# Gate and up products of two token chunks as a 2x2 block product with seven half-depth products in place of eight

## The chip, the cores and the metric

One core of one Trainium2 chip runs the whole program. The metric is device time in microseconds (us): the median of several executions. Beside it stands one profiled execution, whose records every row below comes from. The engines are PE (TensorE matmul; PEld is its weight load), DVE (VectorE), ACT (ScalarE), POOL (GpSimd) and SP (SyncE, which issues the DMAs here). A matmul accumulates into one of eight PSUM banks of 128 x 512 floats.

## The reference

A pre-norm transformer block with 2048 tokens, model width 448, 16 heads of 28, a sliding attention window of 256, and a gated feed-forward of width 1792:

```python
x = A_x                                   # (1, 2048, 448)
h = x + attention(layernorm(x), A_wqkv, A_wo)
n = layernorm(h)
g = n @ B_w_gate                          # 448 -> 1792
u = n @ B_w_up                            # 448 -> 1792
out = h + (gelu_tanh(g) * u) @ B_w_down   # 1792 -> 448
```

## The kernel before, in words

**High and low parts.** Every float32 operand is held as two rounded parts, `hi` and `lo = x - hi` (`to_hi` on ACT, `to_lo` on DVE or POOL), and a product is the sum of hi·hi, lo·hi and hi·lo. The model width 448 is three blocks of 128 rows and one of 64. `xT` holds the normalised tokens with the model width on the partitions: blocks 0 to 2 hi, block 3 with the last 64 rows' hi in one half and their lo in the other, blocks 4 to 6 lo. `TERMS` lists the eleven pairs (weight part, weight block, token block) that make one product of a 128-wide tile of `B_w_gate` or `B_w_up` with a chunk of 512 tokens:

```python
TERMS = [(0, 0, 0), (0, 1, 1), (0, 2, 2), (0, 3, 3), (0, 0, 4), (0, 1, 5), (0, 2, 6),
         (1, 0, 0), (1, 1, 1), (1, 2, 2), (1, 3, 3)]
```

**The attention stage** projects q, k, v, computes scores, takes maxima, exponentials and the weighted sum, and ends with the output projection (`output`). `attend` (L894) runs its matmuls in column tiles of 32 (`tile_position=(0, 32 * j)`), everything else in that stage on the full array.

**The feed-forward stage** (`feed_forward`, `product`) has 56 products: 14 tiles of the feed-forward width times 4 chunks of 512 tokens, in groups of 3, 4, 4 and 3 tiles (`GROUPS`). A product computes gate and up for its tile and chunk (two banks), then gelu (ACT, L1125), the gating product (DVE, L1127), the hi and lo parts of the result (`proj`), and the down product: for each of four blocks of 128 tokens three terms of 448 columns, accumulated over the group in four banks, and at the end of a group added to `hres` (L1158).

- The first four products (`n < PAIRED`) are done "whole": 2 x 11 matmuls over 128 partitions and 512 columns. They are also what fills the end of the attention stage.
- The other 52 are done "paired": each matmul over 128 partitions is cut into two halves of 64 rows with `tile_position` (0, 0) and (64, 0), of which one works for the gate bank and one for the up bank at the same time (`pair`). Phase 0 has ten such pairs and phase 1, with the halves exchanged, eleven, since a term of only 64 rows then takes its place beside another one: 21 pairs in place of 22 whole matmuls. The down products of all 56 but the last are paired too, 12 pairs each, in two phases of six.
- Two halves that work at the same time must write different banks. Where a bank changes from one half to the other, `seen` (L1068, tile `word`) makes ACT read one element of the bank after the last matmul of the first half, and the first matmul of the other half waits for that.
- In the paired stretch the two phases of a gate/up product alternate with the two phases of an earlier down product, so that a phase lies between one `seen` and the matmul that waits for it. `feed_forward` writes this order out by a chain of dependencies.

**Order.** All instructions are recorded first (`Lists.op`, with a cost, a latency and a key), and a planner (`Lists.refine`, a random search with `SEED` and `ROUNDS`, then `Lists.run`) writes out one order for each engine. Its costs know nothing of tile modes. `mul` (L484) issues nearly all matmuls, `to_hi` is L487 and `to_lo` L490, so rows are told apart by tiles and shapes. Weights of a tile arrive by one DMA and are cut in hi and lo into one of seven slots (`RECS`): two in `proj`, one in `rq`, two in `rk`, two in `rec`. So `xT,rk` in a row of the profile is a gate/up product whose weights lie in `rk`, and `rec,proj` a down product with weights in `rec`.

Of the kernel before, what the change touches and what calls it, by code (L numbers as in the profile page):

```python
# [25 lines left out]
GROUPS = [3, 4, 4, 3]  # L26
REC = 2944
NB = NG * CS
# [12 lines left out]
LEAD = 110  # L41
# [3 lines left out]
SWAP = -60  # L45
# [3 lines left out]
AHEAD = 7  # L49
BEHIND = 5  # L50
# [3 lines left out]
PAIRED = 4  # L54
MOVED = 0
SPANS = {"pp", "proj", "raw", "xT", "h", "rqf", "rkf", "vm", "rec0", "rec1", "rec2"}
# [13 lines left out]
ROUNDS = 220  # L70
SEED = 33
# [295 lines left out]
def block_kernel(ctx: ExitStack, tc, x, wqk_in, wv_in, wo_in, ffn_in, out):  # L367
# [16 lines left out]
    xT = pool.tile([128, 7, S], F32R, name="xT")  # L384
    rq_m = pool.tile([128, 4096], F32R, name="rq")
    rk_m = pool.tile([128, 6144], F32R, name="rk")
# [7 lines left out]
    last_hi = pool.tile([128, 128], F32R, name="lasthi")  # L394
# [28 lines left out]
    def open_rec():  # L423
        fst.close()
        p = ctx.enter_context(tc.tile_pool(name="fp", bufs=1))
        rec.extend(p.tile([128, REC], F32R, name=f"rec{i}") for i in range(2))
        rec.append(p.tile([128, S], F32R, name="xh"))


    rq = [rq_m[:, 2048 * u:2048 * u + 2048].rearrange("p (j t) -> p j t", j=4) for u in range(2)]  # L430
# [141 lines left out]
    def turn(t, key):  # L572
        c = slice(t * 128, (t + 1) * 128)
        d = xn_d[t]
        xb, at = (v_m[:, REC:REC + D], span("vm", REC, D)) if t > 7 and t % 2 else (xn[1], ("xn", 1))
        op("dve", 0.56, 0.65, key, lambda: nc.vector.transpose(xb, xn[0]), [("xn", 0)], [at], port=True)
        for a in range(4):
            dst = d.rearrange("(b i) t -> i b t", i=32)[:, :, 32 * a:32 * a + 32]
            src = xb[32 * a:32 * a + 32].rearrange("i (b t) -> i b t", t=32)
            dma(key, 150, lambda dst=dst, src=src: nc.sync.dma_start(dst, src), [at], [("xnd", t, a)])  # L580
        put = [("xnd", t, a) for a in range(4)]
# [13 lines left out]
        op("act", 0.7, 0.82, key + 0.2, hi, [("xt3", t)], [XT(t), "lasthi"])  # L595
        op("dve", 0.75, 0.82, key + 0.2, lo, [XT(t), "lasthi"], [XT(t)], port=True)
# [357 lines left out]
    def flat(m, name, o):  # L954
# [5 lines left out]
    RECS = [(lambda o=o, m=m, name=name: flat(m, name, o), flat(m, name, o)[1], need) for m, name, o, need in (  # L960
        (proj_m, "proj", 0, None), (proj_m, "proj", REC, None), (rq_m, "rqf", 0, "ringfree"),
        (rk_m, "rkf", 0, "ringfree"), (rk_m, "rkf", REC, "ringfree"))] + \
        [(lambda i=i: flat(rec[i], f"rec{i}", 0), flat(rk_m, f"rec{i}", 0)[1], "fp") for i in range(2)]
    GH = [(proj_m, 2 * REC + 1024 * i) for i in range(2)]
    NR = len(RECS)
# [8 lines left out]
    def weight_at(i):  # L974

        q = 0 if i < 3 else i % 3
        raw, at0, name = raw_m[:, 0:1472], 0, "raw"
        if q:
            raw, at0, name = v_m[:, 1472 * (q - 1):1472 * q], 1472 * (q - 1), "vm"
        return raw, at0, name  # L980
# [5 lines left out]
    def weight_splits(i, key, after=()):  # L986
        raw, at0, name = weight_at(i)
        cut = ((0, 512), (512, 512), (1024, D))
        get, rat, opened = RECS[i % NR]
# [16 lines left out]

    def feed_forward():  # L1010
        first = [4 * sum(GROUPS[:gi]) + k for gi, gn in enumerate(GROUPS) for k in range(gn)]
        loaded = split = -1
        n = 0
        for gi, gn in enumerate(GROUPS):
            for c in range(4):
                down = [Bank(("down", i)) for i in range(4)]
                for k in range(gn):
                    i = sum(GROUPS[:gi]) + k
                    while loaded < 2:
                        loaded += 1  # L1020
                        split += 1
                        weights(loaded, 16 * NB + 5 * loaded if loaded < 2 else FFN + 30 * first[loaded] - 20)
                    if n == PAIRED:
                        for cc in (1, 2, 3, 0):
                            cs = slice(512 * cc, 512 * cc + 512)
                            dma(FFN + 30 * PAIRED - 25 + cc, 128, lambda cs=cs: nc.sync.dma_start(
                                f(rec[2][64:128, cs]), f(xT[0:64, 3, cs])), [span("xT", 4 * cc, 4), "fp"], [("xh", cc)])
                    product(n, i, c, k, gn, gi, down)
                    while split < NF - 1 and first[split + 1] <= n + BEHIND:
                        split += 1  # L1030
                        weight_splits(split, FFN + 30 * first[split] - 20, phase[n][0][0:1])
                    while loaded < NF - 1 and first[loaded + 1] <= n + AHEAD:
                        loaded += 1
                        if loaded < 3:
                            split += 1
                            weights(loaded, FFN + 30 * first[loaded] - 20, phase[n][0][0:1])
                        else:
                            weight_load(loaded, FFN + 30 * first[loaded] - 20, phase[n][0][0:1])
                    n += 1

        todo = [h for m in range(n) for h in (down_a[m], down_b[m])]
        order = [todo.pop(0) for _ in range(4)]
        for m in range(PAIRED, n):
            for ph in phase[m]:
                order += [ph, todo.pop(0)]
        order += todo
        order = [o for part in order for o in part]
        for o, last in zip(order, [None] + order):
            for d in [last] if last else whole:
                if d not in o.deps:  # L1050
                    o.deps.add(d)
                    d.users.append(o)

    row = {}
    down_a, down_b, phase, whole = {}, {}, {}, []
    HALF = (slice(0, 64), slice(64, 128))

    def pair(key, n, lat, a, b, r, banks):

        def go():  # L1060
            for x, (bk, w, m, start, stop) in enumerate((a(), b())):
                mul(bank[bk.k][:, 0:n], w, m, start=bool(start), stop=bool(stop),
                                 tile_position=(64 * x, 0), skip_group_check=True)
        return op("pe", mm(n), lat, key, go, r, (), banks)

    def seen(key, b):

        op("act", 0.08, 0.17, key, lambda: nc.scalar.activation(word[0:1, 0:1], bank[b.k][0:1, 0:1], AF.Copy), (),  # L1068
           (), b)

    def product(n, i, c, k, gn, gi, down):
        get, rat, _ = RECS[i % NR]
        key = FFN + 30 * n
        toks = slice(c * 512, (c + 1) * 512)
        early = n < EARLY
        paired = n >= PAIRED
        bs = []
        for q in range(0 if paired else 2):

            turn = 2 * (n - EARLY) + q + (2 if n == 2 else -2)  # L1080
# [4 lines left out]
            for a, (h, wb, xb) in enumerate(TERMS):  # L1085
                whole.append(op("pe", mm(512), 0.403, key + (SWAP if n == 3 else 0) + q * NP + a / NP, lambda a=a, h=h, wb=wb, xb=xb, q=q, b=b: mul(
                    bank[b.k], get()[0][q][h][:, wb, :], xT[:, xb, toks], start=(a == 0), stop=(a == NP - 1)),
                   [span("xT", 4 * c, 4), *rat[q][h]], (), b, tag="early" if early else None))
        if paired:
# [226 lines left out]
```

## Time and profile before

| what | us |
|---|---|
| median of 3 runs (698.36 to 698.57) | 698.57 |
| the profiled execution's own time | 698.08 |
| its span, first to last instruction | 696.4 |
| PE busy | 687.8 (99%) |
| DVE, ACT, POOL busy | 396.9, 362.4, 158.7 |
| granted TensorE clock, mean | 0.999 |

The span is what the rows of the trace divide up; 1.68 us lie around it. A busy share of an engine is an average over stages: POOL, for instance, is idle in nearly all of the feed-forward stage. A matmul's row gives its start and a modelled duration that is longer than the distance to the next start, since matmuls are pipelined; the price of one is therefore read from the distance between the starts of rows. Two halves of a pair start together and are two instructions.

### The profile page before, as it was taken

Reading aid. Unit: us, or ns where it says so; the run is one execution under the profiler, and the core shown is the slowest. Engines: PE = TensorE matmul, PEld = TensorE weight load, DVE = VectorE, ACT = ScalarE, POOL = GpSimd, SP = SyncE. Lnnn points to the kernel's source line nnn. Section 1 sums busy time; section 2 is a strip of 40 time slices with the busy share of each in tenths; the row PEclk is TensorE's granted clock in tenths of the full one; section 3 lists DMA queues with packets and bytes.
Section 4 is the critical chain, followed back from the end, with each engine's and each line's share of the span. In section 5 each row is a group of like instructions: output and inputs, shape, how many; then the busy total and the mean of one; then the engine's idle time right before and its main releaser. Section 6 shows DMA issues by size and latency. Waiting matters only on the chain.

```text
span 696.4 us, 15402 instructions
## 1 busy us (share of the span) xinstructions
PE 687.8 (99%) x5897; PEld 604.7 (87%) x5897; DVE 396.9 (57%) x1057; ACT 362.4 (52%) x930; POOL 158.7 (23%) x253
## 2 busy tenths in 40 slices
PE   8999999999999999999999999999999999999997
PEld 8998888888888887778899999999999999999996
DVE  7987877876687978877764232245232244333224
ACT  7658767776767888896653222234222234222221
POOL 5604434344454653753100000000000000000000
PEclk9999999999999999999999999999999999999999
DMA  8888647475556688524663000012100000001012
GB/s 297 262 282 243 210 150 229 141 213 164 176 168 197 160 247 226 157 55 95 146 188 131 1 2 2 1 44 88 45 1 2 1 1 2 1 1 55 10 45 106
DMA packets 83138, 79.12 MB, mean 114 GB/s; under 512 B 34104, under 2 KB 72952, under 8 KB 83064
## 3 DMA queue, kind: packets, MB, share of 16 engines
q1 hardware_dynamic: 83064, 78.14, 37.4%
q8 instruction: 46, 0.75, 0.4%
q14 instruction: 28, 0.23, 0.1%
HBM read 48.23 MB, written 29.36 MB: 111 GB/s over the span
## 4 chain that ended last, share of the span: by engine, by line
PE 91%; ACT 3%; DVE 3%; issue 1%; POOL 1%; DMA 0%; DVEq 0%; ACTq 0%
PE bank L484 85%; PE bank L894 5%; PE bank L542 1%; ACT pp L864 1%; ACT xn L537 1%; ACT xT L487 1%; DVE bnst L519 1%; ACT rq L487 0%; DVE xT L490 0%; DVE mt L792 0%; DVE hres L941 0%; POOL bnve L511 0%; PE bank L819 0%; DMA hres<-in_x_dram 0%; ACT proj L487 0%
## 5 line engine op out<-in xcount | busy, mean ns | idle before, releaser
L484 PE MATMUL bank<-xT,proj 64*128 64x512 f32 (+1 forms) x907 | 177.1, 381 | 0.0
L792 DVE CUSTOM_DVE_ANT_0 mt<-bank,mt 128x384 bf16<-128x384 f32 (+2 forms) x256 | 129.4, 528 | 34.4 <-PE bank L484 29.4
L864 ACT ACTIVATE pp<-bank 128x384 f32<-128x384 f32 (+2 forms) x352 | 124.1, 390 | 44.8 <-PE bank L484 39.1
L484 PEld LDWEIGHTS bank<-xT,proj 64*128 64x128 f32 (+1 forms) x907 | 118.6, 188 | 11.9 <-issue 0.8
L1127 DVE TENSOR_TENSOR mt<-bank,mt 128x512 f32<-128x512 f32 x54 | 37.2, 688 | 129.3 <-ACT mt L1125 129.3
L875 POOL TENSOR_SCALAR_AFFINE_SELECT pp<-pp 128x512 f32<-128x512 f32 x120 | 75.6, 643 | 114.3 <-ACT pp L864 109.6
L484 PE MATMUL bank<-rq,rk 104*128 104x384 f32 (+2 forms) x352 | 97.3, 297 | 0.8 <-ACT pp L864 0.4
L1125 ACT ACTIVATE mt<-bank 128x512 f32<-128x512 f32 x54 | 32.2, 596 | 108.5 <-PE bank L484 108.5
L484 PE MATMUL bank<-rk,rq 84*128 84x384 f32 (+2 forms) x256 | 81.5, 333 | 0.6 <-DVE proj L490 0.5
L1068 ACT ACTIVATE word<-bank 1x1 f32<-1x1 f32 x162 | 25.4, 157 | 106.7 <-PE bank L484 106.4
L484 PEld LDWEIGHTS bank<-rq,rk 104*128 104x128 f32 x352 | 65.5, 189 | 14.3 <-ACT pp L864 4.0
L484 PE MATMUL bank<-xT,rk 64*128 64x512 f32 x656 | 77.7, 376 | 0.0
L484 PE MATMUL bank<-xT,rec 64*128 64x512 f32 x656 | 77.7, 376 | 0.0
L484 PEld LDWEIGHTS bank<-xT,rec 64*128 64x128 f32 x656 | 63.6, 186 | 7.2
L484 PEld LDWEIGHTS bank<-xT,rk 64*128 64x128 f32 x656 | 63.6, 186 | 7.2
L1158 DVE TENSOR_TENSOR hres<-bank,hres 128x448 f32<-128x448 f32 x64 | 35.5, 617 | 59.5 <-ACT mt L1125 33.8
L484 PE MATMUL bank<-proj,xT 128*128 128x224 f32 x352 | 58.0, 275 | 0.0
L490 DVE TENSOR_TENSOR proj<-mt,proj 128x512 fp32r<-128x512 f32 x54 | 37.3, 692 | 35.7 <-ACT proj L487 30.7
L484 PEld LDWEIGHTS bank<-rk,rq 84*128 84x128 f32 x256 | 48.1, 190 | 8.3 <-issue 2.9
L484 PEld LDWEIGHTS bank<-proj,xT 128*128 128x128 f32 x352 | 51.8, 191 | 0.9
L484 PE MATMUL bank<-wos,ohl 128*128 128x448 f32 x192 | 51.4, 365 | 0.2 <-DVE mx L792 0.2
L487 ACT ACTIVATE proj<-mt 128x512 fp32r<-128x512 f32 x54 | 34.0, 629 | 31.0 <-DVE mt L1127 30.0
(109 smaller groups left out, 967.6 us busy)
## 6 DMA issues: line engine op xcount, KB each, us to landing
rk<-k SPq DMA_DIRECT2D x44, 336.0 KB
rq<-q SPq DMA_DIRECT2D x32, 336.0 KB
q<-proj SPq DMA_DIRECT2D x15, 448.0 KB
raw<-in_ffn_dram SPq DMA_DIRECT2D x7, 736.0 KB
v<-in_ffn_dram SPq DMA_DIRECT2D x7, 736.0 KB
k<-proj SPq DMA_DIRECT2D x11, 448.0 KB
hres<-in_x_dram SPq DMA_DIRECT2D x16, 224.0 KB
out_dram<-hres SPq DMA_DIRECT2D x16, 224.0 KB
```

Source lines behind the costliest of these rows:

```text
L484: nc.tensor.matmul(o.rearrange("p (t h) -> p t h", h=2), w, mixed(m), **how)
L487: nc.scalar.activation(dst, src, AF.Copy)
L490: (eng or nc.vector).tensor_sub(dst, src, f(hi))
L519: op("dve", 0.65, 0.63, key(t), lambda t=t: nc.vector.bn_stats(bnst[t % 2], hres[:, t, :]), [HR(t)], [("bnst", t % 2)])
L792: nc.vector.tensor_tensor_reduce(plain(junk[s % 2][:, o:384]), unmixed(bank[b.k][:, o:384]), plain(mask[:, o:384]), 1.0, -BIG, OP.add, OP. ...
L864: nc.scalar.activation(plain(pp[:, j, o * 128:o * 128 + n]), unmixed(bank[b.k][:, 0:n]), AF.Exp, scale=SCALE)
L875: nc.gpsimd.affine_select(a, a, pattern=[[0, 4], [-cm, 128]], compare_op=op_, fill=0.0, base=0, channel_multiplier=cm)
L894: nc.tensor.matmul(bank[b.k][32 * j:32 * j + DH + 1, lo * 128:(hi + 1) * 128], v[:, 4 * c - 2 + m, g % 2, j, :], pp[:, j, at[m] * 128:(at[ ...
L1068: op("act", 0.08, 0.17, key, lambda: nc.scalar.activation(word[0:1, 0:1], bank[b.k][0:1, 0:1], AF.Copy), (), (), b)
L1125: op("act", 0.485 + table, 0.608 + table, key + NP, lambda: nc.scalar.activation(plain(g2), src(0), AF.Gelu_apprx_tanh), held[0], G2, bs[0 ...
L1127: op("dve", 0.605, 0.702, key + 2 * NP, lambda: nc.vector.tensor_tensor(plain(g2), src(1), plain(g2), op=OP.mult), [*G2, *held[1]], G2, bs ...
L1158: op("dve", 0.533, 0.626, key + 2 * NP + 3 * q + 3, lambda t=t, b=down[q]: nc.vector.tensor_tensor(plain(hres[:, t, :]), unmixed(bank[b.k] ...
```

## The change

The first eight products (chunks 0 and 1, tiles 0 to 3) stay in the old form, all of them whole now (`conv`). The other 48 become 24 units. A unit takes one tile and two chunks of 512 tokens, and computes gate and up for both: a 2x2 block product, since the model width without its last 64 rows is cut in two depths of 192 rows (rows 0 to 127 with 256 to 319, and 128 to 255 with 320 to 383). It uses the seven products of Strassen and Winograd, named P1 to P7, in place of eight. The last 64 rows ("11", "12", "21", "22") are multiplied in the usual way.

- The sums and differences of the token blocks are made once (`combine`: DMA from the transposed tokens in DRAM, four DVE additions and the hi/lo parts for each 128 tokens of a pair of chunks, kept in `xT` and a new tile `X0`). Those of the weights are made for each loaded tile (`record`: five POOL subtractions, hi parts on ACT, lo parts on DVE and POOL, into one of three slots of the ring; 18 loads, since six of the units use the tiles of the two before them).
- Each P is four matmuls over 128 partitions (hi·hi, lo·hi, hi·lo, and one with 64 rows of hi and of lo together) and one of 64 rows; each of the last-row products is one over 128 partitions and one of 64 rows. The 64-row ones stand in two-by-two `rest` steps with a `tile_position` between the matmuls over the full array; that of P7 stands alone.
- Results are put together by one ACT copy and five DVE additions out of four banks, then two gelus, two gating products and two hi/lo splits. Down products keep the paired form, but both phases of one now follow each other, with their two `seen`s.
- Also: `rq`, `rk` and `rec` become one tile `ring` and `X0`; `LN2` gives new keys to the second layer norm; `SEED` is 1 and `ROUNDS` 200.

The core of the diff:

```diff
-GROUPS = [3, 4, 4, 3]
+RS = 3840
+GC = 4
+FIRST = ((0, 0), (0, 1), (1, 0), (1, 1), (0, 2), (0, 3), (1, 2), (1, 3))
+SEGS = ((0, (4, 5)), (0, (6, 7)), (0, (8, 9)), (1, (8, 9)), (1, (6, 7)), (1, (4, 5)), (1, (0, 1)), (1, (10, 11)), (0, (10, 11)), (0, (12, 13)), (1, (12, 13)), (1, (2, 3)))
...
-PAIRED = 4
...
+    PEEL = {"11": (0, 0, 0, LOW), "12": (1, 0, 1, LOW), "22": (1, 1, 1, HIGH), "21": (2, 1, 0, HIGH)}
+    BANK = {"P1": 0, "P2": 0, "11": 0, "P6": 1, "P7": 2, "22": 2, "P4": 2, "21": 2, "P5": 3, "P3": 3, "12": 3}
...
+    def full(name):
+        return [[(name, 0)]] if name in PEEL else [[(name, a)] for a in range(4)]
+
+    def rest(*names):
+        return [[(name, 1 if name in PEEL else 4) for name in names]]
+
+    PART1 = full("P1") + full("P6") + rest("P1", "P6") + full("P7") + rest("P7") + full("22") + full("P5") + rest("P5", "22")
+    PART2 = full("P2") + full("11") + full("P4")[:1] + rest("P2", "P4") + full("P3")[:1] + rest("11", "P3") + [3] + \
+        full("P4")[1:] + full("21") + rest("12", "21") + full("P3")[1:] + full("12")
...
+    def unit(n, p, j):
...
+        def play(steps, out, key):
+            for m, step in enumerate(steps):
+                if step == 3:
+                    seen(key + 0.2 * m, bs[3])
+                    continue
...
+                def go(items=items):
+                    for i, w, x, row, start in items:
+                        how = {} if row is None else dict(tile_position=(row, 0))
+                        mul(bank[bs[i].k], w, x(), start=start, stop=False, skip_group_check=True, **how)
...
+        play(PART1, part1[n], key)
+        op("act", 0.49, 0.605, key + 2, lambda: nc.scalar.activation(plain(A), unmixed(bank[bs[0].k]), AF.Copy), (), ta, bs[0])
+        add(key + 3, A, ta, A, ta, 1)
+        add(key + 4, Bt, tb, A, ta, 2)
+        add(key + 4, Bt, tb, Bt, tb, 3)
+        yield
+        play(PART2, part2[n], key + 8)
+        add(key + 12, C, tc_, A, ta, 2)
+        add(key + 13, A, ta, A, ta, 3)
...
+        for n, (s, p, k, j) in enumerate(units):
...
+            chain.extend(part1[n])
+            if n != 1 and n < len(units) - 1:
+                next_down()
...
+            chain.extend(part2[n])
+            if n:
+                next_down()
```

`next_down` puts the 12 pairs of one down product into the chain.

512 lines of the change are left out of this document (365 added, 147 removed).

## The prediction

> **What bounds the kernel now.** I read the page first (busy times, the chain), then the stretch of the paired products in the view by windows, then single rows of the timeline.
>
> ```profile
> span 696.4 us, 15402 instructions
> PE 687.8 (99%) x5897; PEld 604.7 (87%) x5897; DVE 396.9 (57%) x1057; ACT 362.4 (52%) x930; POOL 158.7 (23%) x253
> PE 91%; ACT 3%; DVE 3%; issue 1%; POOL 1%; DMA 0%; DVEq 0%; ACTq 0%
> 332.53 358.43 PE bank L484 x3467
> 333.20:689.64 356.44, 356.44 (x3458) 326.71 (x3456) 131.40 (x218) 110.39 (x315) 1.48 (x4) 1.00 0.13 39
> ```
>
> The fourth line is the longest piece of the chain: from 332.53 us on nothing but matmuls sets the end, for 358 us. The fifth (PE, PEld, DVE, ACT, POOL busy, clock) says the same of the paired stretch: PE is never idle, DVE works 131 of 356 us, ACT 110, POOL not at all. So in the stage that is changed the time is the number of TensorE slots times the price of one, and there is room on the other engines. The price is the distance between starts:
>
> ```profile
> 666.78 2.32 PE L484 MATMUL bank<-xT,rk 64*128 64x512 f32 x20
> 668.94 1.30 PE L484 MATMUL bank<-rec,proj 64*128 64x448 f32 x12
> 670.07 2.53 PE L484 MATMUL bank<-xT,rk 64*128 64x512 f32 x21
> 672.23 0.38 PE L484 MATMUL bank<-xh,rk 64*128 64x512 f32 x1
> 672.45 1.30 PE L484 MATMUL bank<-rec,proj 64*128 64x448 f32 x12
> 673.58 0.38 PE L484 MATMUL bank<-xT,rec 64*128 64x512 f32 x2
> ...
> 317.81 4.05 PE L484 MATMUL bank<-xT,rq 128*128 128x512 f32 x18
> 321.70 1.49 PE L484 MATMUL bank<-wos,ohl 128*128 128x448 f32 x7
> ```
>
> Ten pairs of 512 columns take 668.94 - 666.78 = 2.16 us, 0.216 each; six pairs of 448 take 1.13, 0.188 each; a product (21 and 12 pairs) 6.80. A whole matmul of 512 columns costs the same as a pair: 3.89 / 18 = 0.216. Between pairs of different shape nothing is lost.
>
> **Slots removed.** Before, the feed-forward has 4 x 22 + 52 x 21 = 1180 slots of 512 columns. After, 8 x 22 = 176 for the first products; a unit has in its first part 4 + 4 + 1 + 4 + 1 + 1 + 4 + 1 = 20 and in its second 4 + 1 + 1 + 1 + 1 + 1 + 3 + 1 + 1 + 3 + 1 = 18, so 38 in place of the 42 of two products, and 24 x 38 = 912. Together 1088: 92 fewer, worth 92 x 0.216 = 19.9 us. The order of instructions of the built program has these counts. Down slots are the same number as before. It is not an eighth, because the last 64 rows do not take part and the seven 64-row remainders fill slots badly.
>
> **What is added on TensorE: changes of tile mode.** Before, whole matmuls are followed by half-array pairs once, at 327 us, and the other way once, at the end. After, the `rest` steps and the paired down products stand between full-array matmuls: seven stretches of halves in each unit (one fewer in unit 0, which has no down product behind it) and six around the first products, 173 in all by the order of instructions, each with a change in and a change out. That is 346 changes against 2. What one costs is seen at the end of the trace, where no semaphore is waited for:
>
> ```profile
> 689.46 0.35 PE L484 MATMUL bank<-rec,proj 64*128 64x448 f32 x2
> 689.74 0.46 PE L484 MATMUL bank<-rec,proj 128*128 128x448 f32 x1
> 690.22 0.54 PE L484 MATMUL bank<-rec,proj 128*128 128x448 f32 x2
> 689.74 0.19 PEld L484 LDWEIGHTS bank<-rec,proj 128*128 128x128 f32 x1 [0.28 <-issue]
> ...
> 301.35 0.27 PE L484 MATMUL bank<-rq,rk 104*128 104x256 f32 x1
> 301.55 0.15 PEld L894 LDWEIGHTS bank<-pp,v 128*29 128x29 f32 x8 [0.20 <-issue]
> ...
> 277.32 0.48 PE L484 MATMUL bank<-xT,proj 128*128 128x512 f32 x1
> ```
>
> The last pair starts at 689.46; the next slot was due 0.19 later, at 689.65. The weight load of the first full-array matmul (last line of the first four) starts only at 689.74, after idling for "issue", where in the steady stretch it runs beside the matmul before: 0.09 lost. Then that matmul takes 0.46 instead of 0.35, since its weights come in while nothing else runs: two steps from 689.74 to 690.22 are 0.48, not 0.38, another 0.10. Together 0.19 to 0.20. The change in the other direction isn't to be had free of a semaphore in this trace (at 327.19 it waits for `proj`). The nearest are the changes between the full array and the 32-column tiles of `attend`: into them a matmul of 256 columns takes 0.20 until the next load starts, and by the step from 448 to 512 columns (0.028 for 64) it should take 0.11, so 0.09 again, with "issue"; out of them the first matmul takes 0.48 where those inside a run have about 0.38. Both kinds thus show both losses, and I take 0.20 for a change in either direction: 344 x 0.20 = 68.8 us. Ends: 0.09, if the reload can be hidden, and 0.22, by the largest reading of both losses (0.10, and 0.48 against 0.36).
>
> The Trainium skill, "TensorEngine Tiling (Array Packing)", Key Properties, says that changing the tiling mode, as against only the tile, drains the TensorE. It speaks against this change and names no price; by the drain alone, at this trace's 0.09, the sum below would be 712, by the rows 750.
>
> **Waits in the down products.** Before, one phase of another product lies between a `seen` and the matmul that waits for it. Now both phases of a down product follow each other, with three pairs (0.57 us) as cover. Where the trace has that order it shows this:
>
> ```profile
> 329.70 2.55 PE L484 MATMUL bank<-proj 64*128 64x448 f32 x24 [0.23 <-ACT word L1068]
> 332.53 0.83 PE L484 MATMUL bank<-proj 64*128 64x448 f32 x6 [0.28 <-ACT word L1068]
> ...
> 688.40 0.68 PEld L484 LDWEIGHTS bank<-rec,proj 64*128 64x128 f32 x8 [0.27 <-ACT word L1068]
> ```
>
> The first two down products and the last paired one run so: six waits, three of them late. The last lets PEld idle 0.27 where the step is 0.19, and adds a reload of 0.10: 0.18. The 55 paired down products have two such waits each: between 0 and 110 x 0.18 = 20 us. In the order of ACT's instructions in the units, the two `word`s of a down product follow each other with at most one long instruction between them, and nothing long that comes due late stands just ahead, so I take the low side: 3 us, for the crowded places around the first products.
>
> **Work on the other engines.** Prices:
>
> ```profile
> L1127 DVE TENSOR_TENSOR mt<-bank,mt 128x512 f32<-128x512 f32 x54 | 37.2, 688 | 129.3 <-ACT mt L1125 129.3
> L490 DVE TENSOR_TENSOR proj<-mt,proj 128x512 fp32r<-128x512 f32 x54 | 37.3, 692 | 35.7 <-ACT proj L487 30.7 <-ACT word L1068 4.9
> L1158 DVE TENSOR_TENSOR hres<-bank,hres 128x448 f32<-128x448 f32 x64 | 35.5, 617 | 59.5 <-ACT mt L1125 33.8 <-PE bank L484 25.7
> L487 ACT ACTIVATE proj<-mt 128x512 fp32r<-128x512 f32 x54 | 34.0, 629 | 31.0 <-DVE mt L1127 30.0
> L490 POOL TENSOR_TENSOR ohl<-oT,ohl 128x512 fp32r<-128x512 f32 x15 | 19.2, 1279 | 4.6 <-ACT ohl L487 2.7 <-PE bank L484 1.9
> ```
>
> Per unit DVE has five additions, two gating products and two splits, 9 x 0.69 = 6.2 us, four additions into `hres` on average, 2.5, and about 1.4 for the weights: 10.1. ACT has five of 0.63, some `word`s and the weights' hi parts, about 6. POOL has some 6.7 per loaded tile (five subtractions of half the size at about 0.65 and seven low parts), 5 per unit on average. A unit is 38 x 0.216 + 24 x 0.188 + 14 x 0.20 = 8.2 + 4.5 + 2.8 = 15.5 us. All of it hides, also under the 12.7 that a unit would be without the changes of mode. The banks come round in time too: the second part's P4 needs bank 2 read twice by DVE (1.4 us), and 12 down pairs (2.3 us) stand before it. `combine` for the first unit is some 17 us of DVE; after the attention six of the first eight products with their downs, over 45 us, cover it; if that fails it is the head of unit 0 that waits, a few us once. The attention stage gets another random order: I count 0, with 3 us to each side. The DMAs (two per loaded tile) run in a stage with the share 0.13 in the window above.
>
> **Sum**, against the profiled execution: 698.08 - 19.9 + 68.8 + 3 = 750.0; the median of the runs before is 0.5 above it, so 750 for the median: two products in unit form 15.5 where they had 13.6.
>
> **Rivals.**
> - Only one of the two losses is paid: the load of the next weights slips under the end of the other mode's matmul (or only changes out of halves cost). 344 x 0.09 = 31 or 172 x 0.20 = 34: 698 - 20 + 31 to 34 + 3 = 712 to 715. Against it: both kinds of change seen above show the long first matmul. The Trainium skill, "TensorE: Matmul & The Clock Gate", The mechanism (Part 3), says that PE pulls a weight load ahead of running matmuls where row groups don't conflict or it goes to the background buffer; by that rule this rival would win, and the row at 689.74 does not bear it out.
> - Faster: a change of mode costs nothing when it is in a steady stream, and what is seen at 689.74 belongs to the tail. Then 698 - 20 + 3 = 681, with DVE still hidden (10.1 of 12.7). It decides from 19.9 / 344 = 0.058 us per change: below that the change gains. For it: there is just one such row; against it: the two rows of `attend`.
> - The waits for `word` are late in most down products, since ACT has new evacuations to do: the whole 20 us, 698 - 20 + 69 + 20 = 767.
>
> **How the numbers follow.** Forecast 0.78, at 750; half price 0.09, at 713; free 0.06, at 681; late waits 0.07, at 767. The forecast's own spread comes from the price (0.17 to 0.22 is 10 us down and 7 up), the waits, and the attention's order: 737 to 766. That leaves out the first two rivals and a little at the top, 0.2 in all. Faster by over 0.2% (1.4 us, about what a measurement of this kernel can tell from no change) is the second rival, 0.06; the same 0.01; slower 0.93.
>
> **What would show it.** In the trace after: `issue` as the releaser of well over 150 idle times of PEld on full-array loads; a first full-array matmul after each stretch of halves with 0.48 instead of 0.38; starts of equal places of two neighbouring units 15.5 us apart. 12.7 apart would prove the second rival, 14 the first. Few PE rows should wait for DVE or POOL. Wrong would be a unit that is long because PE waits for weights or for evacuations, with the changes of mode free.

## The result and the profile after

The changed kernel takes 756.9 us (median of 4 runs, 755.41 to 758.36) against 698.47 (698.12 to 698.57) for the kernel before, run beside it: a ratio of 1.084, 95% interval 1.0815 to 1.086, so 58 us or 8.4% slower. The forecast was 750, its range 737 to 766. The profiled execution of after took 757.33 us, its span 755.6.

The page of after: the span, the busy times, and the shares of the chain that ended last.

```profile
span 755.6 us, 14186 instructions
PE 743.8 (98%) x4836; PEld 565.9 (75%) x4836; DVE 569.6 (75%) x1381; ACT 420.7 (56%) x1046; POOL 306.6 (41%) x469
PE 85%; DVE 8%; ACT 4%; issue 2%; DMA 1%; POOL 0%; DVEq 0%; SPq 0%; ACTq 0%
```

TensorE has 1061 instructions fewer than before and is busy 56 us longer, while its weight loads are busy 39 us less. What the extra time is, the busy times don't say; the distances between starts do. The timeline of after, PE and then PEld, over about one unit (start, duration, engine, operation, and in brackets the idle time before it and its releaser):

```profile
601.81 0.38 PE L488 MATMUL bank<-X,proj 128*128 128x512 f32 x1
602.12 2.55 PE L488 MATMUL bank<-ring,proj 64*128 64x448 f32 x24
604.60 0.70 PE L488 MATMUL bank<-xT,ring 128*128 128x512 f32 x2
605.14 0.38 PE L488 MATMUL bank<-X,ring 128*128 128x512 f32 x1
...
620.14 0.70 PE L488 MATMUL bank<-xT,proj 128*128 128x512 f32 x2
...
617.65 2.20 PEld L488 LDWEIGHTS bank<-ring,proj 64*128 64x128 f32 x24 [0.33 <-DVE v L1246]
620.13 0.30 PEld L488 LDWEIGHTS bank<-xT,proj 128*128 128x128 f32 x2 [0.28 <-issue]
```

Into the halves: 0.31 us from 601.81 to 602.12 where a step of 512 columns is 0.216, so 0.09 lost. Out of them: the 12 pairs of 448 columns need 12 x 0.189 = 2.27, and 604.60 is 2.48 after 602.12, so 0.21 for the slow first pair and the way out. The first two whole matmuls then take 0.54 in place of 0.43: another 0.10 to 0.11. Equal places of two units, 604.60 and 620.14, lie 15.54 us apart; the forecast said 15.5.

The waits of PEld and of PE behind the attention stage (us in total, times, longest):

```profile
PEld bank L488 <- issue: 73.5, 268, 0.3
PEld bank L488 <- ACT v L1258: 7.0, 21, 0.3
PEld bank L488 <- DVE v L1246: 6.5, 20, 0.3
PEld bank L488 <- DVE hres L1312: 6.1, 23, 0.8
...
PE bank L488 <- DVE hres L1312: 0.5, 1, 0.5
PE bank L488 <- ACT ohl L491: 0.2, 1, 0.2
```

The busy times in two stretches (PE, PEld, DVE, ACT, POOL, granted clock, DMA share, GB/s):

```profile
322.00:480.00 158.00, 156.77 (x916) 113.70 (x910) 139.38 (x286) 83.42 (x204) 63.34 (x96) 1.00 0.34 93
480.00:752.00 272.00, 271.63 (x1613) 189.72 (x1609) 179.28 (x286) 96.17 (x253) 88.53 (x132) 1.00 0.13 44
```

The 268 waits for `issue` of 0.27 each are changes of mode. Most of the next three rows are changes too: a mean of 0.27 to 0.33 is a change's idle time, put down to whichever semaphore came last. The four rows count 332 idle times; there are 346 changes. Matmuls themselves wait for 0.7 us in all. So PE is "busy" throughout, and the loss lies inside what the page calls busy.

To find what remains, I split each span at the last matmul of `attend`. In the timeline of before the last of these 24 starts at 316.86:

```profile
315.63 1.50 PE L894 MATMUL bank<-pp,v 128*29 128x384 f32 x24
```

In that of after the last of these 20 starts at 322.03:

```profile
321.14 1.16 PE L981 MATMUL bank<-pp,v 128*29 128x384 f32 x20
```

Behind it the slots are counted in the order of the built program and priced at 0.216 (512 columns) and 0.189 (448 columns), each change at 0.198; what is left over up to the start of the last matmul is "waits". So "waits" holds the idle time and also the steps that ran at a lower granted clock behind a wait. The end after that is 4.3 to 4.8 us in all of them.

| profiled execution | last `attend` | slots behind it | changes | waits | span |
|---|---|---|---|---|---|
| before | 316.9 | 372.8 | 0.4 | 1.9 | 696.4 |
| after | 322.0 | 355.5 | 68.5 | 5.2 | 755.6 |
| difference | +5.2 | -17.3 | +68.1 | +3.3 | +59.2 |

Of the 92 slots that the change saves, 80 (17.3 us) are saved behind the last `attend`; the other 12 mean that after has done 2.6 us less of matmuls by then, and is 5.2 later all the same.

### The profile page after: what moved, and what is told of

It is laid out like the page before. It is cut to its first block, busy times and chain, and to the rows that moved or that the text cites. A ratio compares the mean times of both kernels' runs of the same rounds, so it can differ in the third digit from the quotient of the medians.

```text
span 755.6 us, 14186 instructions
## 1 busy us (share of the span) xinstructions
PE 743.8 (98%) x4836; PEld 565.9 (75%) x4836; DVE 569.6 (75%) x1381; ACT 420.7 (56%) x1046; POOL 306.6 (41%) x469
## 4 chain that ended last, share of the span: by engine, by line
PE 85%; DVE 8%; ACT 4%; issue 2%; DMA 1%; POOL 0%; DVEq 0%; SPq 0%; ACTq 0%
PE bank L488 79%; PE bank L981 5%; DVE xT L494 2%; DVE X L494 1%; ACT pp L951 1%; ACT ring L491 1%; ACT xT L491 1%; DVE v L656 1%; DVE hres L1312 1%; DVE proj L494 1%; DVE mt L879 1%; ACT xn L541 1%; PE bank L546 0%; DMA v<-xn 0%; DMA hres<-in_x_dram 0%
## 5 line engine op out<-in xcount | busy, mean ns | idle before, releaser
L488 PE MATMUL bank<-xT,proj 128*128 128x512 f32 (+1 forms) x620 | 194.9, 405 | 1.1 <-DVE xT L494 1.1
L488 PE MATMUL bank<-xT,ring 128*128 128x512 f32 (+1 forms) x536 | 171.6, 420 | 0.1
L1246 DVE TENSOR_TENSOR v<-v,bank 128x512 f32<-128x512 f32 x120 | 82.4, 687 | 97.6 <-PE bank L488 79.3
L488 PE MATMUL bank<-ring 84*128 84x384 f32 (+4 forms) x608 | 152.2, 315 | 2.1 <-ACT ring L491 1.3
L488 PEld LDWEIGHTS bank<-xT,proj 128*128 128x128 f32 (+1 forms) x620 | 109.6, 191 | 32.6 <-issue 20.1
L488 PE MATMUL bank<-ring,proj 64*128 64x448 f32 x1236 | 130.9, 356 | 0.8 <-DVE hres L1312 0.5
L488 PEld LDWEIGHTS bank<-xT,ring 128*128 128x128 f32 (+1 forms) x536 | 90.5, 187 | 52.9 <-issue 39.9
L488 PEld LDWEIGHTS bank<-ring 104*128 104x128 f32 (+1 forms) x608 | 108.6, 192 | 23.1 <-issue 4.9
L488 PEld LDWEIGHTS bank<-ring,proj 64*128 64x128 f32 x1236 | 109.1, 185 | 19.2 <-DVE v L1246 6.0
L488 PE MATMUL bank<-X,ring 128*128 128x512 f32 (+1 forms) x240 | 90.5, 413 | 0.0
```

The lines of the kernel that those rows point to most:

```text
L488: nc.tensor.matmul(o.rearrange("p (t h) -> p t h", h=2), w, mixed(m), **how)
L1246: op("dve", 0.605, 0.702, key, lambda: nc.vector.tensor_tensor(plain(out), plain(a), unmixed(bank[bs[i].k]), op=OP.add), ar, w, bs[i])
```

## The experiments

The theory (A) is the prediction's: what is lost are changes between half-array and full-array matmuls, 0.198 us each in either direction. The rivals are that the changes are free or half that price, and that TensorE waits for `word` or for the evacuations. The same split for the experiments, from their profiled executions, beside the median times:

| kernel | median us | ratio to before (95%) | last `attend` | slots | changes (number) | waits | span |
|---|---|---|---|---|---|---|---|
| before_whole_down | 743.4 | 1.0628 (1.0612 to 1.0644) | 322.6 | 372.6 | 41.2 (208) | 0.0 | 740.7 |
| after_whole_down | 743.7 | 1.0633 (1.0617 to 1.0649) | 317.7 | 354.5 | 57.0 (288) | 7.5 | 741.5 |
| after_two_stretches | 730.6 | 1.0444 (1.0413 to 1.0475) | 326.4 | 355.5 | 21.4 (108) | 22.2 | 730.4 |
| after_no_mode_change | 701.5 | 1.0046 (1.0029 to 1.0063) | 324.4 | 353.4 | 0 (0) | 16.6 | 698.7 |
| after_one_combine | 690.6 | 0.9883 (0.9861 to 0.9906) | 321.7 | 355.8 | 0 (0) | 7.2 | 689.0 |
| before_other_plan | 702.3 | 1.0043 (1.0027 to 1.0059) | 324.9 | 372.2 | 0.4 (2) | 1.5 | 703.4 |
| after_other_plan | 762.6 | 1.0922 (1.0886 to 1.0958) | 328.2 | 352.9 | 68.5 (346) | 10.6 | 764.6 |
| full_array_units | 716.6 | 1.0258 (1.0231 to 1.0286) | 316.9 | 364.2 | 0 (0) | 30.6 | 716.2 |
| full_array_early | 714.7 | 1.0218 (1.0184 to 1.0251) | 316.0 | 361.2 | 0 (0) | 33.1 | 714.6 |
| full_array_pool | 718.0 | 1.0279 (1.0258 to 1.0299) | 321.3 | 360.9 | 0 (0) | 29.3 | 715.9 |
| full_array_pool_lo | 736.9 | 1.0548 (1.053 to 1.0566) | 321.5 | 364.4 | 0 (0) | 44.3 | 734.7 |
| full_array_pool_lo8 | 724.9 | 1.0378 (1.0362 to 1.0394) | 324.3 | 361.2 | 0 (0) | 33.1 | 723.0 |

Every edit changes the recorded program, so the planner draws a new order; the column "last `attend`" moves with that too.

### The changes alone, in the kernel before: before_whole_down

```diff
-            for j in range(2):
+            for q in (2 * ph, 2 * ph + 1):
...
-                    (down_b if ph else down_a)[n].append(pair(...))
-                if not ph:
-                    seen(key + 2 * NP + 3 * j + 3, down[2 * j + 1 - k % 2])
+                    (down_b if ph else down_a)[n].append(op("pe", mm(D), 0.38, ..., lambda ...: mul(
+                        bank[down[q].k][:, 0:D], gh(oh)[:, q, :], get()[0][2][wh], ...)))
```

> The kernel before with its down products done as whole 128-row matmuls between the paired gate and up phases: the same number of slots (1488 of 512 columns and 864 of 448), no reads into word in the down products, and 208 changes of mode in place of 2. Nothing else of the change is in it. Theory A (0.198 us a change): 206 x 0.198 = 40.8 us more, less about 1 for reads into word: 738 us (736 to 741) against 698.5. Rival B (changes free): 697 to 699. Rival C (half price, or one direction only): 718.

Measured: 743.4 us, 5 above the expectation, 44 above the kernel before beside it (699.2). The timeline in the paired stretch:

```profile
601.34 0.38 PE L484 MATMUL bank<-xh,rq 64*128 64x512 f32 x1
601.65 1.40 PE L484 MATMUL bank<-proj 128*128 128x448 f32 x6
602.98 2.43 PE L484 MATMUL bank<-xT,rk 64*128 64x512 f32 x20
605.34 1.40 PE L484 MATMUL bank<-proj 128*128 128x448 f32 x6
```

Six whole matmuls take 1.33 from start to start where 6 x 0.189 is 1.13, ten pairs take 2.36 where ten steps are 2.16: 0.20 for each run of either kind. Each of these 0.20 is the slow first step of a change in one direction and the way out of a change in the other. The two parts can be told apart: from the last pair (601.34) to the first whole matmul is 0.31 where a step is 0.216, so 0.09 is lost on the way out of the halves, as after lost 0.09 on the way into them. Over all 208 changes of this trace the step before a change is 0.094 too long on the way in and on the way out, and the step behind it 0.104 too long in both: one direction costs as much as the other. 208 x 0.198 is 41.2, and with it the waits behind the attention come out at 0.0. Both cheap rivals fall. The 5 us that the expectation missed are the attention stage, which ends 5.7 later here, though the edit touches nothing in it.

### Fewer changes in the kernel after: after_whole_down

```diff
-        for ph in range(0 if ends else 2):
-            for jj in range(2):
...
-                    res.append(pair(...))
-                if not ph:
-                    seen(key + 3 * jj + 3, banks[2 * jj + 1 - k % 2])
+        for q in range(0 if ends else 4):
+            for a, (oh, wh) in enumerate(PARTS):
+                res.append(op("pe", mm(D), 0.38, ..., lambda ...: mul(
+                    bank[banks[q].k][:, 0:D], gh(oh)[:, q, :], R[wh], ...)))
```

> The kernel after with every paired down product done as whole 128-row matmuls (the same number of 448-column slots) and without its two reads into word; the rest steps keep their halves. 288 changes of mode in place of 346, by the order of the built program. Theory A, each change costs 0.198 us (0.094 until the weight load starts, 0.104 of load that nothing covers, as the trace after shows in both directions): 58 x 0.198 = 11.5 us less, and 1 to 3 us of word waits less: 742 to 745 us against 756.9. Rival B, the 68 us are matmuls that wait for ACT's reads into word, and the changes cost nothing: all these reads but those of the units' second part are gone, so under 700 us. Rival C, only half of the price is paid: 749 to 752.

Measured: 743.7 us, inside the expectation, but by other terms than expected: 58 changes fewer are 11.5 us, the attention ended 4.3 earlier with 1 us fewer slots behind it, and waits rose by 2.3 although nearly all reads into `word` were gone. Those reads were not what cost time (rival B said under 700).

### Two stretches of halves in a unit: after_two_stretches

```diff
-    PART1 = full("P1") + full("P6") + rest("P1", "P6") + full("P7") + rest("P7") + full("22") + full("P5") + rest("P5", "22")
+    PART1 = full("P1") + full("P6") + full("P7") + full("22") + full("P5") + rest("P1", "P6") + rest("P7") + rest("P5", "22")
-    PART2 = full("P2") + full("11") + full("P4")[:1] + rest("P2", "P4") + full("P3")[:1] + rest("11", "P3") + [3] + ...
+    PART2 = full("P2") + full("11") + full("P4") + full("21") + full("P3") + full("12") + rest("P2", "P4") + rest("11", "P3") + [3] + rest("12", "21")
...
-            chain.extend(part2[n])
+            chain.extend(part2[n][:-1])
...
+            chain.append(part2[n][-1])
```

> The kernel after with the rest steps of each part gathered at its end, beside the paired down product, so that a unit has two stretches of halves in place of seven: the same matmuls, the same number of slots, all reads into word, 108 changes of mode in place of 346. Theory A (0.198 us a change): 238 x 0.198 = 47.1 us less, 710 us (706 to 714; about 2 us to each side for waits, as the 64-row steps now stand closer to the evacuations of their banks). Rival B (waits for word, changes free): no gain, 755 to 760. Rival C (half price): 733.

Measured: 730.6 us, 26 less than after and 21 more than expected. The changes fell by their 47.1 us, but waits rose from 5.2 to 22.2 and the attention ended 4.4 later. The waits of PEld from 330 to 726 us:

```profile
PEld bank L488 <- issue: 29.8, 96, 0.3
PEld bank L488 <- DVE v L1246: 6.4, 11, 1.1
PEld bank L488 <- ACT word L1215: 5.5, 12, 1.0
PEld bank L488 <- DVE proj L494: 3.1, 4, 1.2
PEld bank L488 <- ACT v L1250: 2.8, 4, 1.3
PEld bank L488 <- DVE hres L1312: 2.6, 3, 1.9
```

`issue` went from 268 times to 96; now single waits of 1 to 2 us for DVE and for `word` stand there. It may be that the changes had covered them; but the edit also puts the 64-row steps closer to the evacuations of their banks, and no run separates the two.

### No change at all: after_no_mode_change

```diff
-                return R["pl"][rows, l], lambda: XP(p)[rows, x], r + at("pl", l), rows.start
+                return R["pl"][:, l], lambda: XP(p)[:, x], r + at("pl", l), None
...
-        return R["bl"][rows, blk], x(1, rows), [XS(p, q, 1)] + at("bl", blk), rows.start
+        return R["bl"][:, blk], x(1), [XS(p, q, 1)] + at("bl", blk), None
...
-                for name, a in step:
+                for name, a in step[:1]:
```

and the down products as in after_whole_down.

> The kernel after with no half-array matmul in the feed-forward at all: down products whole as in the first run, and each rest step replaced by one matmul over 128 rows with the operands of its first name, which leaves the other name's 64-row term out of the sum. The same number of 512-column slots (1396) and 448-column slots (864), 0 changes in place of 346. Theory A: 346 x 0.198 = 68.5 us less and 1 to 3 us of word waits less: 685 to 688 us, so 10 to 13 under the kernel before, where 92 slots of 0.216 are 19.9; the rest of that sits in the attention stage (about 5.5 us longer after) and in waits around the first units. Rival B (waits for evacuations and weights, not for the array): the evacuations and the loads are as they were, so over 740. Rival C (half price): 720.

Measured: 701.5 us. With all 346 changes gone it is 55 us less than after, not 69 to 72, and the kernel is still not faster than before, although it leaves terms out. Equal places of two units lie 12.74 us apart, against 15.54 in after; over 14 changes a unit that is 0.200 for each:

```profile
596.25 2.43 PE L488 MATMUL bank<-ring,proj 128*128 128x448 f32 x12
608.99 2.43 PE L488 MATMUL bank<-ring,proj 128*128 128x448 f32 x12
```

From 480 us on PE never waits; the missing time lies earlier. The windows of this kernel:

```profile
324.00:480.00 156.00, 144.72 (x692) 128.22 (x685) 145.81 (x297) 82.32 (x163) 66.59 (x99) 0.99 0.33 93
480.00:694.00 214.00, 214.00 (x1047) 197.40 (x1046) 170.45 (x273) 84.51 (x158) 90.65 (x128) 1.00 0.17 55
```

And three groups of DVE between 340 and 470 us (busy, mean ns | idle before), which are the work of `combine`:

```profile
L494 DVE TENSOR_TENSOR xT<-v,xT 64x256 fp32r<-64x256 f32 (+1 forms) x26 | 12.0, 463 | 0.3
L494 DVE TENSOR_TENSOR X<-v,xT 128x256 fp32r<-128x256 f32 (+1 forms) x26 | 11.3, 436 | 0.0
L656 DVE TENSOR_TENSOR v<-v 128x256 f32<-128x256 f32 x20 | 10.7, 537 | 0.2
```

DVE is busy 146 of 156 us while PE idles 11 of them. I formed a second theory: with the changes gone, DVE is the bound of the first units, because `combine` for the second pair of chunks comes on top of the units' own work.

### Without combine for the second pair: after_one_combine

```diff
-        for i in range(4):
-            combine(1, i, FFN + XK[1][0] + XK[1][1] * i)
...
         R, at, _ = rec_of(j)
+        p = 0
```

> The run without changes of mode, with one more edit: combine for the second pair of chunks is left out, and the units of that pair read the sums of the first pair (their outputs are those of other tokens). TensorE's instructions are the same; about 25 us of DVE additions and low parts between 380 and 470 us are gone. Theory A (in that run DVE is the bound of the first units, 49.5 busy of 50 us from 400 to 450): of its 16.6 us of waits behind the attention only those before and in unit 0 stay (4 to 7): 689 to 693 against 701.5, with some us to each side for the planner's draw in the attention. Rival B (the waits come from the weights or the evacuations of each unit): 699 to 703.

Measured: 690.6 us, 10.9 less than the run above, as theory A said. Waits fell from 16.6 to 7.2; the earlier end of the attention (2.7) and the slots then left behind it (2.4) cancel out. So `combine` for the second pair cost about 9 us of TensorE's time. The edit takes its DMAs and ACT's hi parts out too; that it is DVE's share that binds is read from the window above (146 of 156 us) and from the waits of PE in the run above from 340 to 500 us, 8.5 of 8.8 us for DVE. This is also the first of these kernels below the one before, but with work left out.

### The planner's draw: before_other_plan and after_other_plan

```diff
-ROUNDS = 220
-SEED = 33
+ROUNDS = 200
+SEED = 1
```

in before, and the reverse in after.

> The kernel before with SEED 1 and ROUNDS 200 for its planner, as the kernel after has them; no matmul is added or taken away. It asks where the 5 us come from by which the attention stage of after is longer. The last matmul of attend starts at 316.9 us in before, at 322.0 in after and, in the four edits above, between 317.7 and 326.4. Theory A (the planner's draw, not the change): before with another draw ends its attention 1 to 9 us later too, 700 to 708. Rival B (the work that the change puts beside attention): 697 to 699.5.

> The kernel after with SEED 33 and ROUNDS 220, as the kernel before has them; the same matmuls and the same 346 changes of mode. Theory A (the draw): the end of attend moves by some us either way, 752 to 761. Rival B (the change's own work lengthens the attention stage): 756 to 758 again. In both, the units lie 15.5 us apart.

Measured: before 702.3, which is 0.43% (0.27 to 0.59) slower by the draw alone, inside what theory A said; its profiled execution, the slowest of its runs at 705.15, ends `attend` 8.1 later than before, with a granted clock of 0.66 from 130 to 140 us in it. After 762.6, 6 slower, somewhat beyond the range that was given. So the draw moves these kernels by 4 to 6 us, and the order in which the kernel before runs its attention is the better one of its two. That the change's own work adds nothing to that stage isn't shown by this: the last matmul of `attend` starts between 316.9 and 324.9 us in the three orders of before, and between 317.7 and 328.2 in the six orders with the units of after, which overlap.

### A version with all terms and no halves: full_array_units

```diff
-    PART1 = full("P1") + full("P6") + rest("P1", "P6") + ...
-    PART2 = full("P2") + full("11") + ...
+    def full(name):
+        return [[(name, a)] for a in range(6 if XQ[name] in JOIN else 5)]
+    PART1 = full("P1") + full("P6") + full("P7") + full("P5")
+    PART2 = full("P2") + full("P4") + full("P3")
...
+        if a == 4:
+            return R["bl"][:, w], x(1), [XS(p, q, 1)] + at("bl", w), None
+        k = JOIN[q][0]
+        return R["hi"][:, w, 1], lambda: X2(p, k), [XS(p, 7, k)] + at("hi", w), None
```

For room in SBUF, `combine` for the first pair lost its second buffer and the layer norm of the later tokens took its place.

> The block product of after, whole, with no half-array matmul at all. The 64-row pieces of two terms that go to one bank (P2 with 11, P3 with 12, P7 with 22, P4 with 21) lie in one 128-row operand, hi parts in one tile and lo parts in another, so that three whole matmuls do what two whole ones and two halves did; P1, P6 and P5 get whole matmuls with 64 rows of zeros among their weights. 39 slots a unit (1420 of 512 columns in all, 68 fewer than before), down products whole, 0 changes of mode. Theory A (the price of the changes, and DVE as the next bound in the first units, where combine for the second pair of chunks comes on top of the units' own work): attention to 317 to 326, 361 of slots behind it, 14 to 20 of waits as in the run without changes, 6 for the ends: 699 to 713, about 705. Rival B (the waits of that run came from its missing steps): 685 to 692, the full worth of 68 slots (14.7). Rival C (half-array changes were never the cause): near 760.

Measured: 716.6 us, 3.6 above the upper end. The units run at 39 slots without a gap behind 480 us, as meant, but 30.6 us of waits stand ahead of that, against 16.6 in the run without changes. The worst, in the timeline of PE:

```profile
380.79 1.22 PE L486 MATMUL bank<-xT,proj 128*128 128x512 f32 x2 [10.28 <-ACT xT L489]
381.80 0.63 PE L486 MATMUL bank<-X,proj 128*128 128x512 f32 x1
382.23 1.06 PE L486 MATMUL bank<-xT,proj 128*128 128x512 f32 x2
...
390.66 0.46 PE L486 MATMUL bank<-X,proj 128*128 128x512 f32 x1
390.96 0.60 PE L486 MATMUL bank<-xT,proj 128*128 128x512 f32 x2
```

10.28 us for the sums of `combine`, and then the steps are 0.427 (381.80 to 382.23) in place of 0.216 until 390.9. The 18 matmuls from 380.79 to 390.66 cost some 3.8 us more by this, on top of the wait.

### Four attempts to take the load off DVE

The first, full_array_early, restores the second buffer, records the layer norm of the later tokens behind it, puts eight units of the first pair ahead, and runs the additions for the second pair on POOL; full_array_pool has `ADDS = ("pool", "pool")`.

```diff
-SEGS = ((0, (4, 5)), (0, (6, 7)), (0, (8, 9)), (1, (8, 9)), ...
+SEGS = ((0, (4, 5)), (0, (6, 7)), (0, (8, 9)), (0, (10, 11)), (1, (10, 11)), (1, (8, 9)), ...
-XK = ((0, 10), (240, 10))
+XK = ((0, 10), (270, 14))
-ADDS = ("dve", "dve")
+ADDS = ("dve", "pool")
...
-        other = p
+        other = p or i % 2
```

> The units without half-array matmuls, all terms in, with four edits of order alone: combine for the first pair alternates between two buffers again, since the layer norm of the later tokens is recorded behind it; eight units of the first pair of chunks come first in place of six (20 tiles loaded in place of 18); combine for the second pair is due 30 us later; and its additions run on POOL. Theory A (DVE bound in the first units): of the 30.6 us of waits of the first such kernel, 10.6 in one wait for combine's xT at 366 us, 10 to 22 go: 695 to 707. Rival B (the sums for the first units come no earlier): 714 to 718.

> The same with the additions of combine for the first pair on POOL too: 16 additions of some 0.54 us less for DVE ahead of unit 0, 16 of some 0.75 more for POOL. Theory A: if DVE's work bounds unit 0's start, 1 to 6 us less than the run before it; if the chain of one token tile (DMA, additions, hi, lo) bounds it, the slower additions make it the same or up to 4 us more.

Measured: 714.7 and 718.0. The first is what rival B said. The second is 3.3 more than the first, which fits the chain of one token tile as the bound, but a draw alone moves these kernels by as much. The waits stayed at 33.1 and 29.3 us. The last two put more of DVE's work on POOL (full_array_pool_lo8 keeps the eight units first, with `LOP` up to 11 and `(180, 40)`):

```diff
-LOP = ()
+LOP = (0, 1, 2, 3, 4, 5, 6, 7, 8, 9)
-XK = ((0, 10), (270, 14))
+XK = ((0, 10), (180, 25))
```

> The first kernel of full-array units with the buffers and the order of the layer norm of full_array_early, its segments as in after (18 tiles loaded), and more of DVE's work on POOL: the additions of combine for the second pair, and the low parts of al and d of the first ten loaded tiles (2.5 us of DVE a tile); combine for the second pair spread over more units. Theory A (DVE's total work up to 500 us is the bound): some 25 us less for DVE there, so 10 to 20 of its 30 us of waits go: 697 to 708. Rival B (the order of the work, the chain of one token tile and POOL's slower parts bound it): 710 to 720.

> The same with eight units of the first pair of chunks first (20 tiles loaded, the low parts of twelve of them on POOL), which gives combine for the second pair some 100 us of units to hide in, in place of 76. Theory A: 695 to 706, below the run before it. Rival B: 710 to 720.

Measured: 736.9 and 724.9: worse than every range. Two DVE groups from 340 to 500 us in full_array_units, and the windows of that stretch:

```profile
L492 DVE TENSOR_TENSOR proj<-v,proj 128x512 fp32r<-128x512 f32 x16 | 12.5, 799 | 0.2
L492 DVE TENSOR_TENSOR X<-v,xT 128x256 fp32r<-128x256 f32 x22 | 9.9, 452 | 0.5 <-ACT xT L489 0.2
```

```profile
340.00:500.00 160.00, 141.09 (x630) 123.36 (x629) 145.85 (x305) 80.99 (x174) 69.93 (x107) 0.91 0.27 75
```

The same of full_array_pool_lo:

```profile
L492 DVE TENSOR_TENSOR proj<-v,proj 128x512 fp32r<-128x512 f32 x12 | 13.7, 1164 | 1.3 <-ACT proj L489 1.1
L492 DVE TENSOR_TENSOR X<-v,xT 128x256 fp32r<-128x256 f32 x23 | 14.6, 637 | 1.2 <-ACT xT L489 0.8
```

```profile
340.00:500.00 160.00, 129.51 (x563) 110.46 (x563) 134.63 (x245) 80.44 (x173) 108.17 (x163) 0.90 0.29 76
```

POOL worked 38 us more, and in these two groups DVE's own instructions took 41 to 46% longer: with 60 instructions fewer DVE was busy only 11 us less. The units' additions, whose second input is a PSUM bank, didn't lengthen (681 and 684 ns); the last section says what sets the two kinds apart. No version here beats the kernel before with all of its work done. How these first 160 us should be ordered so that 68 saved slots pay is left open.

## Why the prediction was right, point by point

- **Slots and their price.** 92 fewer at 0.216: right. A unit without changes takes 12.74 us in after_no_mode_change, its slots times their prices (38 x 0.216 + 24 x 0.189).
- **The changes of mode.** 344 more at 0.20 were to be 68.8 us; by the split they are 68.1. The split takes its 0.198 from the trace of after; the 0.200 from the units of after and after_no_mode_change, and the 208 changes of before_whole_down, don't depend on it. One row at the end of the trace of before had shown both losses, and the direction into the halves, only bounded by the rows of `attend`, costs the same. Of the first rival's reading, that the next weights slip under the end of the other mode's matmul, nothing is seen in either direction. The Trainium skill, "TensorE: Matmul & The Clock Gate", "Step-by-step: what each phase is for" (Part 2), has PE load the next tile's weights while this tile's matmul runs, where the row groups don't conflict or the load goes to the background buffer. The trace agrees inside a mode and not across a change of it, where the first step is 0.10 longer each time.
- **Waits, 3 us.** 3.3 by the split; the number agrees by luck, since they are not where the prediction put them: `word` isn't among the releasers that matter. They are single waits around the first units, most of them for DVE.
- **The attention stage, 0 with 3 to each side.** This is the mis-sized term: 5.2 later with 2.6 us of matmuls less done, 7.8 in all, against the 7.3 us by which the forecast of the profiled execution fell short (757.33 for 750.0). The draws of before_other_plan and before_whole_down move the same point by 8.1 and 5.7 with no work added there, so a draw is enough to explain it. In all three the clock has a part in it. The windows of before and then of after:

```profile
280.00:290.00 10.00, 9.90 (x72) 7.98 (x72) 9.01 (x30) 9.68 (x28) 8.57 (x10) 1.00 0.55 137
280.00:290.00 10.00, 8.51 (x29) 7.15 (x30) 5.71 (x21) 7.91 (x23) 6.35 (x9) 0.66 0.52 129
```

  In after PE waits for 0.60 and 1.34 us (the second up to 282.97), and the granted clock is 0.50 for 6.8 us, in which PE is busy for 6.5: about 3.2 us lost. before_other_plan and before_whole_down have such stretches of 6.8 and 3.4 us in this stage, before has none. The spread should have been 4 us (by the medians of before and before_other_plan) to 8 us (by the profiled executions) upward: of the three orders of that program's attention seen here, before has the earliest.
- **"All of it hides, also under the 12.7".** Wrong, and without effect on the forecast only because the changes were there. The count of 10.1 us of DVE in a unit was about right (170.45 us for the last 214 of after_no_mode_change, 10.1 in 12.7), but only the first pair's `combine` was counted, not the second's, which falls among the first units. In after the longer units covered it: DVE 139 of 158 us, PE waiting for 0.7. With the changes gone 16.6 us of waits stand there, and 9.4 of them go when the second pair's `combine` is left out. So the second rival was mispriced: without changes the kernel came out at 701.5, in the one order that was drawn, and not at 681. Of the 20 us between, 11.7 are waits beyond the 3 foreseen and 7.5 the later end of the attention stage.
- **Late waits for word, 767.** Not seen: the two reads of a down product cost little beside the changes, and taking nearly all of them away brought no less waiting.

## What to carry to other kernels

Count the changes between half-array and full-array matmuls in the program's order and price them like slots: here one costs as much as a 448-column matmul, and 346 of them undid 92 saved slots more than three times over. They show in no busy share, only in the distance between starts and in PEld's idle time before `issue`. When a saving makes a bound engine faster, add up the next engine's work in each stage at the new speed, one-off preparations included, before the saving is written down; and with a randomly planned order, take the spread of the plan as a term of its own.

## What the runs showed of the hardware that was not expected

- **A wait of TensorE is followed by slow steps.** After the 10.28 us wait in full_array_units the steps were 0.427 us for the next 10 us, at a granted clock of 0.50 (the windows, PE to POOL, then the clock):

```profile
380.00:384.00 4.00, 2.50 (x5) 1.51 (x5) 3.51 (x12) 3.44 (x8) 0.00 (x0) 0.50 0.76 197
384.00:388.00 4.00, 3.72 (x7) 2.28 (x8) 3.83 (x9) 1.68 (x5) 2.42 (x4) 0.50 0.08 12
...
392.00:396.00 4.00, 4.00 (x21) 3.73 (x20) 4.00 (x7) 0.82 (x3) 1.92 (x3) 1.00 0.54 114
```

  In after_no_mode_change a shorter wait (2.19 us, up to 328.68) did it too:

```profile
328.00:330.00 2.00, 1.32 (x5) 1.04 (x6) 0.69 (x1) 1.97 (x4) 0.00 (x0) 0.83 0.87 322
330.00:333.00 3.00, 3.00 (x10) 2.75 (x9) 2.02 (x4) 3.00 (x6) 0.00 (x0) 0.54 0.66 123
```

  The Trainium skill, "TensorE: Matmul & The Clock Gate", "What's actually happening" (Part 1), has the clock fall to half after an idle window of about 3.4 us and rise after as long a busy one. The trace agrees on the half, though here a wait of 2.2 us was enough, and the slow stretch lasted up to 10 us where short waits went on in it. Behind the attention stage of full_array_units PE is idle for 18.9 us and busy for 17.7 us at a clock of 0.50; half of these, 8.9 us, come on top of the idle time.
- **Work moved from DVE to POOL slows what stays on DVE.** A split of 128 x 512 in SBUF took 799 ns with POOL busy 70 of 160 us and 1164 ns with 108. One by one, the splits that no POOL instruction overlaps in time take 685 ns on average in both traces (9 of 16, and 2 of 12), and the others 947 and 1260. The additions of the units, with one input in a PSUM bank, take 680 to 686 ns with POOL beside them or not. The Trainium skill, "SBUF — State Buffer", section "Who interferes with whom", says that a DVE instruction with two SBUF inputs contends with a POOL instruction that reads SBUF. The traces agree, with 685 ns beside 947 and 1260.
